# Sinkhorn-sorted attention and a gated MLP on one core: K of two batches mixed by 64x64 blocks in four tiles of the array, and a new order of the work

## The chip, the core and the metric

The kernel runs on one core of one Trainium2 chip. A core has a TensorE (PE, which multiplies; its weight loads are listed apart as PEld), a VectorE (DVE), a ScalarE (ACT), a GpSimd (POOL) and a SyncE (SP), which run side by side and wait for each other by semaphores. PE writes into PSUM, eight banks of 128 partitions x 512 floats; DVE and ACT read it. DMA queues move data between memory and the core's SBUF; loads here are issued by POOL, which casts float32 to bfloat16 on the way, and the others by SP and ACT. The metric is the device time of one execution, in microseconds (us), the median of several runs.

## What is computed

Four batches, 8 heads, 768 positions, 64 columns a head. `sort_net` gives an 8x8 matrix P per batch and head, which five Sinkhorn rounds normalise. P mixes the 8 blocks of 96 positions of K and V; attention then stays inside a block; the result goes through a gated MLP whose gate mixes positions.

```python
k_sorted = np.einsum('bhij,bhjcd->bhicd', P, k_b)      # likewise v_sorted
scores = scale * np.matmul(q_b, k_sb.transpose(0, 1, 2, 4, 3))   # 96x96 per block
attn = softmax(scores);  x = attn @ v_sb                # heads side by side: 768 x 512
h = np.maximum(x @ w_in, 0.0);  u, v = h[..., :512], h[..., 512:]
v_s = np.einsum('ts,bsd->btd', w_spatial, layernorm(v)) + b_spatial[None, :, None]
out = (u * v_s) @ w_out
```

## The kernel before

The work is cut into small steps, and one string, `ORDER`, says in which order they are emitted: `KT:3:D:0:1` is step KT in PSUM tile 3, its copy by DVE (A would be ACT), batch 0, head pair 1. Each engine and each queue does its part of the steps strictly in that order; nothing is rescheduled. PSUM tiles 0 to 3 are two banks each, and 10 to 17 are single banks (bank n - 10), so that 14 is the first bank of tile 2.

The steps that the change and the prediction speak of, with their lines:

- `L` (line 171) issues a load on POOL's queue. q, k and v of a batch are 128 partitions x 8 heads x 6 positions x 64 columns: partition p holds positions 6p to 6p + 5.
- `QC` (363) casts the first half of the first batch's q, which SP loads as float32. `QT` (330) turns q of a head pair by PE; for batches 2 and 3 `QP` (369) packs q and `QX` (380) turns it by DMA.
- `SK` (240) is a Sinkhorn round on DVE and ACT. `PR` (263) spreads P over partitions by PE, `P0` (278) on DVE and `PD` (290) on POOL multiply it with a mask into pd: for every head a 128x128 matrix that mixes the 8 blocks, since 128 partitions hold 8 blocks of 16.
- `KT` (402) mixes and turns K of a head pair: 12 matmuls (line 395) of 128 rows x 64 columns of weights (K) and 128 moving columns (pd). Two of them run at once, in the left and the right half of the array. `VT` (405) and `VB` (408) do that with V of batch 0, and turn it back into vb, position by partition.
- `VM` (418) mixes V of the other batches into vm, and `VC` (432) issues SP's DMAs that lay vm out as vb, one for each of the 8 blocks. There are two vb tiles, one for even batches and one for odd.
- `SC` (446) has the scores of a head pair and four blocks: 8 matmuls (454) of 64 rows, and ACT's exponential (459). `AT` (491) multiplies with vb (8 matmuls, 500) and DVE normalises (507, 508). `AT:1:1:0:0` is PSUM tile 1, batch 1, head pair 0, blocks 0 to 3; a last 1 means blocks 4 to 7.
- `XT`, `XD` turn x; `WT`, `WW` turn w_spatial; `VP`, `VH` (559) make the v half of the MLP, `ST`, `LN`, `LA` (581 to 599) its normalisation on DVE and ACT, `UP` (605) the u half, `SP` and `SH` (620, 676) the mixing of positions (PE, then DVE adds the bias), `GT`, `GH` the gate on DVE or POOL, `OP`, `OH` the last product, `OE`, `OI`, `OS`, `OJ` its way out. `CK`, `CF`, `LF` check that a short form of Sinkhorn and softmax was safe; a second path is there if not.

A KT is these lines of `mixed`:

```python
nc.tensor.matmul(
    t[hh * 64:hh * 64 + 64, g * 128:(g + 1) * 128],
    lhsT=st[x, b][:, 2 * hp + hh, g * D:(g + 1) * D], rhs=pd(b)[:, 2 * hp + hh, :],
    start=True, stop=True)
```

Of the kernel before, what the change touches and what calls it, by code (L numbers as in the profile page):

```python
# [30 lines left out]
AT:3:1:3:0 QP:A:2:2 AT:2:1:0:1 QP:A:2:1 SP:0:0:0 AT:1:1:1:1 SP:3:0:2 VM:2:A:2:2 XD:1:0 VM:0:A:2:1 GT:D:0:0 SP:1:0:1
VM:3:D:2:0 GT:P:0:1 VM:2:A:2:3 VH:10:A:1:0 ST:1:0 KT:1:A:2:0 KT:2:D:2:1 KT:3:A:2:3 QX:2:0:4 KT:0:D:2:2 XD:1:1
UP:1:A:1:1:0 VH:16:D:1:1 SC:2:2:2:0 SC:0:2:0:0 VC:2:0:4:0:4 ST:1:1 GT:P:0:2 SC:1:2:3:0 VH:17:D:1:3 L:wo UP:2:A:1:1:1
AT:0:2:2:0 VH:16:A:1:4 AT:1:2:0:0 GT:P:0:3 VH:17:D:1:5 SC:2:2:1:0 L:q:3:0:8 SC:0:2:0:1 SC:1:2:1:1 VH:16:A:1:2 ST:1:3
UP:2:A:1:0:0 ST:1:5 AT:0:2:3:0 ST:1:4 ST:1:2 UP:1:A:1:0:1 LN:1:0:6 OP:3:0:2:2 LA:1:5 LA:1:1 SC:2:2:3:1 L:v:3:0:8
SC:0:2:2:1 PD:3:4:8 LA:1:0 OP:1:0:4:2 PD:3:0:4 LA:1:3 LA:1:2 OE:A:0:2 LA:1:4 L:k:3:0:8 QP:D:3:0 VC:2:4:8:0:4 OE:A:0:4
AT:2:2:3:1 SP:0:1:3 QP:A:3:3 AT:3:2:1:0 AT:1:2:2:1 QP:A:3:1 SP:2:1:1 AT:0:2:1:1 QP:A:3:2 VM:3:A:3:1 OP:1:0:0:2
OE:D:0:0 OS:0:0:0:1:A OS:0:0:1:2:A VM:2:A:3:3 AT:3:2:0:1 SP:0:1:2 VM:1:A:3:0 GT:P:1:1 XD:2:0 VM:3:D:3:2 SP:2:1:0
VH:16:D:2:2 QX:3:0:4 KT:0:A:3:0 KT:1:D:3:2 KT:2:D:3:3 KT:3:A:3:1 XD:2:1 VH:10:D:2:0 SC:1:3:0:1 ST:2:2 SC:3:3:0:0
SC:2:3:3:1 VC:3:4:8:0:4 OS:0:4:0:1 OS:0:4:1:2 VH:11:D:2:4 VH:10:A:2:5 AT:1:3:0:1 GT:P:1:3 VH:16:D:2:3 ST:2:3 ST:2:5  # L40
GT:P:1:2 SC:2:3:1:1 SC:0:3:2:1 SC:1:3:1:0 VH:17:A:2:1 GT:D:1:0 UP:2:A:2:1:0 AT:0:3:2:1 UP:1:A:2:1:1 ST:2:1 AT:3:3:1:1
ST:2:4 AT:2:3:3:1 UP:0:A:2:0:1 ST:2:0 UP:1:A:2:0:0 VC:3:0:4:0:4 AT:3:3:0:0 LN:2:0:6 LA:2:2 OP:0:1:0:2 OE:A:1:0 LA:2:4
# [26 lines left out]
def kernel(  # L69
# [217 lines left out]
    def u_PC(eng):  # L287
        copy(eng, prep_sb, st["pr"])
# [560 lines left out]
```

## Time and profile before

| what | us |
|---|---|
| median of 3 runs | 150.17 |
| lowest and highest | 149.5, 150.21 |
| span of the profiled execution, first to last instruction | 147.7 |
| median less span | 2.5 |

The profiled execution's own time is given by its span; what lies around it is seen only against the timed runs, as the last row does. In the profile a row of the chain or of a timeline begins with the start in us from the span's start and the duration in us; then come the engine, the line and the operation. A line can be a helper's: L122 is every copy by ACT and L124 every copy by DVE. The duration of one matmul in a timeline includes its way through the array, so the pace of a stream of matmuls is read from the chain, whose pieces end where the next begins.

### The profile page before, as it was taken

The page shows a single profiled execution, that of the slowest core. Times are in us where ns is not written, and L with a number is a line of the kernel's source. Part 1 is how long each engine was busy: PE and PEld are TensorE (multiplying, and loading weights), DVE is VectorE, ACT ScalarE, POOL GpSimd, SP SyncE. Part 2 cuts the span into 40 slices and gives each one's busy share as a digit, 9 for nine tenths or more (in the row PEclk, how much of TensorE's full clock was granted, in tenths as well). Part 3 has the DMA queues.
Part 4 walks back from the last instruction along what each step waited for, and adds up shares of the span by engine and source line. Part 5 has one row for each costly group of instructions (what it writes and reads, how often), then busy time and mean ns, then how long its engine had stood idle before and what let it go on. Part 6 is the DMA issues. An engine that isn't in the chain of part 4 may idle for free.

```text
span 147.7 us, 4114 instructions
## 1 busy us (share of the span) xinstructions
PE 141.4 (96%) x1691; PEld 101.0 (68%) x1691; DVE 115.1 (78%) x263; ACT 85.2 (58%) x125; POOL 39.1 (26%) x44
## 2 busy tenths in 40 slices
PE   6997999999999999999999999999999999999991
PEld 2466777857776667776877678768866876854760
DVE  3878899979987978867869879899558989846741
ACT  5357998988789447658793328756640046160040
POOL 6701994410000006991002640000002100004630
PEclk9999999999999999999999999999999999999999
DMA  2999999999999999899999999503602507007856
GB/s 60 278 204 205 204 207 201 208 225 243 227 233 231 204 200 269 131 177 211 206 202 175 213 239 278 132 0 83 28 0 60 190 2 284 0 2 266 307 210 228
DMA packets 37013, 25.93 MB, mean 176 GB/s; under 512 B 16704, under 2 KB 34112, under 8 KB 36992
## 3 DMA queue, kind: packets, MB, share of 16 engines
q0 software_dynamic: 14432, 12.19, 51.9%
q1 hardware_dynamic: 21552, 11.88, 33.8%
q10 hardware_dynamic: 1008, 1.57, 2.8%
q8 instruction: 14, 0.23, 0.6%
q14 instruction: 7, 0.06, 0.1%
HBM read 24.78 MB, written 6.29 MB: 210 GB/s over the span
## 4 chain that ended last, share of the span: by engine, by line
PE 82%; DMA 8%; DVE 5%; POOL 2%; issue 1%; ACT 1%; POOLq 0%; DVEq 0%
PE ps L625 16%; PE ps L567 15%; PE ps L613 14%; PE ps L651 11%; DMA k_in<-in_k_dram 8%; PE ps L681 5%; PE ps L500 4%; PE ps L395 4%; PE ps L701 4%; PE ps L454 4%; PE ps L422 3%; DVE x_sb L508 2%; PE ps L326 1%; PE ps L536 1%; PE ps L530 1%; DVE vb L124 1%
## 5 line engine op out<-in xcount | busy, mean ns | idle before, releaser
L642 POOL TENSOR_TENSOR gt<-z,u_sb 128x768 bf16<-128x768 f32 x7 | 11.4, 1642 | 68.0 <-DVE z L631 54.7
L459 ACT ACTIVATE ex_all<-ps 96x768 bf16<-96x768 f32 x32 | 23.7, 805 | 5.0 <-PE ps L454 4.1
L625 PE MATMUL ps<-wspT,v_sb 128*128 128x384 bf16 x144 | 25.0, 326 | 0.0
L567 PE MATMUL ps<-w_in_sb,xT 128*128 128x256 bf16 (+1 forms) x176 | 23.8, 283 | 0.0
L613 PE MATMUL ps<-xT,w_in_sb 128*128 128x384 bf16 x128 | 23.0, 326 | 0.0
L128 ACT ACTIVATE u_sb<-ps 128x768 bf16<-128x768 f32 x16 | 13.0, 811 | 17.3 <-PE ps L613 17.2
L508 DVE TENSOR_TENSOR x_sb<-ps,rec_all 96x512 bf16<-96x512 f32 x32 | 22.0, 687 | 1.1
L625 PEld LDWEIGHTS <-v_sb 128*128 128x128 bf16 x144 | 13.5, 98 | 8.4
L567 PEld LDWEIGHTS <-xT 128*128 128x128 bf16 x176 | 16.2, 98 | 4.0
L651 PE MATMUL ps<-w_out_sb,gt 128*128 128x256 bf16 x144 | 16.9, 273 | 0.0
L613 PEld LDWEIGHTS <-w_in_sb 128*128 128x128 bf16 x128 | 12.0, 98 | 7.0
L587 DVE BATCH_NORM_STATS2 stats<-v_sb 128x6 f32<-128x512 bf16 x24 | 16.2, 675 | 0.6 <-ACT v_sb L128 0.5
L122 ACT COPY o_sb<-ps 128x1024 f32<-128x1024 f32 (+2 forms) x11 | 8.9, 830 | 12.6 <-PE ps L701 9.3
L631 DVE TENSOR_TENSOR z<-ps,b_bc 128x768 f32<-128x768 f32 x12 | 11.5, 954 | 5.9 <-PE ps L625 5.1
L651 PEld LDWEIGHTS <-gt 128*128 128x128 bf16 x144 | 13.8, 98 | 2.0
L500 PEld LDWEIGHTS <-ex_all 96*128 96x128 bf16 x256 | 11.1, 97 | 2.6
L500 PE MATMUL ps<-vb,ex_all 96*128 96x65 bf16 x256 | 12.4, 193 | 0.1
L122 ACT CAST vm<-ps 128x768 bf16<-128x768 f32 x9 | 6.8, 807 | 9.7 <-PE ps L422 6.6
L694 POOL TENSOR_TENSOR gt<-z,u_sb 128x512 bf16<-128x512 f32 (+1 forms) x5 | 5.2, 1046 | 21.5 <-DVE z L687 21.5
L507 DVE RECIPROCAL rec_all<-ps 96x8 f32<-96x8 f32 x32 | 6.3, 196 | 5.5 <-PE ps L500 5.3
L130 DVE TENSOR_SCALAR v_sb<-ps 128x512 bf16<-128x512 f32 (+1 forms) x12 | 8.7, 727 | 1.7 <-PE ps L567 1.5
L236 PE MATMUL ps<-warm 128*128 128x512 bf16 (+3 forms) x38 | 8.5, 386 | 1.3 <-DVE warm L210 1.3
(100 smaller groups left out, 199.9 us busy)
## 6 DMA issues: line engine op xcount, KB each, us to landing
v_in<-in_v_dram POOLq DMA_DIRECT2D x4, 768.0 KB, 16.0
k_in<-in_k_dram POOLq DMA_DIRECT2D x4, 768.0 KB, 14.9
vb<-vm SPq DMA_DIRECT2D x24, 99.0 KB, 4.8
q_in<-in_q_dram POOLq DMA_DIRECT2D x3, 768.0 KB, 11.6
out_dram<-o_sb SPq DMA_DIRECT2D x9, 256.0 KB, 2.3
out_dram<-o_sb SPq DMA_DIRECT2D x4, 512.0 KB, 5.9
out_dram<-o_sb ACTq DMA_DIRECT2D x5, 256.0 KB, 2.3
ws_in<-in_moe_w_spatial_dram POOLq DMA_DIRECT2D x2, 576.0 KB, 18.9
```

The costliest lines, as they stand in the source:

```text
L122: nc.scalar.copy(out=out, in_=in_)
L128: nc.scalar.activation(out=out, in_=in_, func=AF.Relu)
L459: nc.scalar.activation(out=e_tile(b, hp, ih).rearrange("p h (x g) -> p h x g", g=G), in_=t[0:BLK, :, 0:HW].rearrange("p h (g x) -> p h x g ...
L500: nc.tensor.matmul(t[:, hh, ii * VW:ii * VW + D + 1], lhsT=e[:, c:c + 128], rhs=vb[b % 2][:, ih * NI + ii, 2 * hp + hh, 0:D + 1], start=Tr ...
L508: nc.vector.tensor_mul(out=x_sb[:, hp].rearrange("p i (h d) -> p h i d", h=2), in0=tv[:, :, :, 0:D], in1=_raw_ap(rec, 0, [rec.ap[0], [NI, ...
L567: nc.tensor.matmul(t[:, x, c:c + DH // parts], lhsT=st["xT", b][:, n // 3, kc, (n % 3) * 128:(n % 3 + 1) * 128], rhs=w_in_sb[:, kc, DH + c ...
L587: nc.vector.bn_stats(out=stats, in_=st["v_sb", b, n])
L613: nc.tensor.matmul(t[:, x, 0:HW], lhsT=w_in_sb[:, kc, mc * 128:(mc + 1) * 128], rhs=st["xT", b][:, ih, kc, :], start=(kc == 0), stop=(kc = ...
L625: nc.tensor.matmul(t[:, x, 0:HW], lhsT=st["v_sb", b, n][:, mc * 128:(mc + 1) * 128], rhs=wspT[:, 3 * x:3 * x + 3, n, :], start=(n == 0), s ...
L631: nc.vector.tensor_add(out=z.rearrange("p (x c) -> p x c", x=2), in0=t[:, :, 0:HW], in1=b_bc.rearrange("p (x c) -> p x c", x=2),)
L642: eng.tensor_mul(out=gt, in0=st["z", b, mc], in1=u)
L651: nc.tensor.matmul(t[:, x, c:c + w], lhsT=st["gt", b, mc][:, (n0 + x) * 128:(n0 + x + 1) * 128], rhs=w_out_sb[:, mc, c:c + w], start=(mc = ...
```

## The change

Four things are changed.

1. K of batches 2 and 3 is loaded in another layout: a tile of 128 partitions holds two heads, 64 partitions each, with 12 positions per partition. A head is then mixed by a 64x64 matrix (`pn`, made by POOL in step `PN` from a smaller spread of P, steps `M8`, `PS`, `PY`), and step `KP` does two head pairs at once: 48 matmuls of 64 rows, 64 columns of weights and 64 moving columns, in the four quarters of the array. Four successive matmuls write four different PSUM banks. One KP takes the place of two KT. For odd head pairs the two heads stand in swapped halves, in q too, so their QP is two copies.
2. K of batch 0 is loaded ahead of V, with KT and the first scores ahead of VT.
3. `SH` can write its 512 columns in two parts.
4. `ORDER` is another throughout. Of its table two pieces:

```diff
-S0 TB CO LH:S:0 L:q:0:4:8 SK:0 ... BH ID IV:0 L:v:0:0:8 MC MA SK:1 DM:10:4:256 SK:2
-QC:A:0 SK:3 SK:4 QC:A:1 QT:10:A:0:2 IV:2 QT:11:A:0:3 ...
+S0 TB CO LH:S:0 SK:0 L:q:0:4:8 ... BH L:k:0:0:8 ID IV:0 MC MA M8 SK:1 DM:10:4:256
+SK:2 QC:D:0 SK:3 SK:4 IV:2 QT:11:A:0:0 QC:A:1 ...
```

The core of the rest:

```diff
+        if what == "k" and int(a[0]) >= KB:
+            b, lo, hi = (int(x) for x in a)
...
+            nc.gpsimd.dma_start(
+                out=st["k", b][:, lo:hi],
+                in_=_raw_ap(k, (b * H + 2 * lo) * S * D, [[GR * D, 128], [2 * S * D, hi - lo], [1, GR * D]]),
+            )
...
+    def u_PN(b, lo, hi):
...
+        nc.gpsimd.tensor_mul(
+            out=pn(b)[:, lo:hi].rearrange("p h (i t) -> p h i t", t=TR),
+            in0=_raw_ap(mask8, 0, [mask8.ap[0], [0, n], [0, NB], [1, TR]]),
+            in1=_raw_ap(prep8, (b - KB) * HP + lo, [prep8.ap[0], [1, n], [(B - KB) * HP, NB], [0, TR]]),
+        )
+
+    def half(b, hp, hh):
+        lo = 64 * (hh ^ (hp & 1) if b >= KB else hh)
+        return slice(lo, lo + 64)
...
+    def u_KP(ps0, ps1, eng, b, m):
+        b, m = int(b), int(m)
+        ts = [ps_tile(ps0), ps_tile(ps1)]
+        for n in range(GR):
+            for row in range(2):
+                g = (n + G * row) % GR
+                for o in range(2):
+                    rows = slice(64 * row, 64 * row + 64)
+                    nc.tensor.matmul(
+                        ts[o][half(b, o, row), g // G, (g % G) * 64:(g % G) * 64 + 64],
+                        lhsT=st["k", b][rows, 2 * m + o, g * D:(g + 1) * D], rhs=pn(b)[rows, 2 * m + o, :],
+                        start=True, stop=True,
+                    )
+        for o in range(2):
+            to = turned("kT", b, 2 * m + o)[:, 0:S].rearrange("p (x b g) -> p b x g", b=2, g=G)
+            copy(eng[o], to, ts[o][:, :, 0:HW].rearrange("p b (g x) -> p b x g", g=G))
```

Three places show what the new order moves. The first is ACT's queue in batch 0, from the last turns of q to the first copies of vm (`kt_all` is mixed K, `ex_all` the exponential of the scores, `vt_all` mixed V). Before:

```order
L122 COPY qT<-ps 128x768 x3
L122 CAST vt_all<-ps 128x768
L122 CAST prep_sb<-ps 128x256
L122 COPY vb_97<-ps 96x8x2x64
L122 CAST vt_all<-ps 128x768
L122 CAST kt_all<-ps 128x768 x2
L459 ACTIVATE ex_all<-ps 96x768 x7
```

And in the changed kernel (its line numbers are other ones):

```order
L125 COPY qT<-ps 128x768 x3
L125 CAST kt_all<-ps 128x768 x2
L529 ACTIVATE ex_all<-ps 96x768
L125 CAST vt_all<-ps 128x768
L529 ACTIVATE ex_all<-ps 96x768 x2
L125 CAST vt_all<-ps 128x768
L529 ACTIVATE ex_all<-ps 96x768 x3
L125 CAST vt_all<-ps 128x768
L529 ACTIVATE ex_all<-ps 96x768 x2
L125 CAST vm<-ps 128x2x6x64 x4
```

Mixed K comes first and V between the exponentials; before, V stood ahead of all of them.

The second place is PE's queue where vb of batch 1 is first read; the semaphores DMAHW2 to DMAHW7, then DMAHW0 and DMAHW1, are SP's eight VC in the order of issue. Before, behind a step VH, it is AT:1:1:0:0:

```order
L567 LDWEIGHTS xT
L567 MATMUL ps<-w_in_sb,xT 128x256
L500 LDWEIGHTS ex_all
L500 MATMUL ps<-vb_98,ex_all 128x65 [waits DMAHW2_49]
L500 LDWEIGHTS ex_all
L500 MATMUL ps<-vb_98,ex_all 128x65 [waits DMAHW3_49]
```

In the changed kernel this same step stands behind a VP and waits for the last four:

```order
L637 LDWEIGHTS xT
L637 MATMUL ps<-w_in_sb,xT 128x512
L570 LDWEIGHTS ex_all [waits DMAHW6_49]
L570 MATMUL ps<-vb_101,ex_all 128x65 [waits DVE_49]
L570 LDWEIGHTS ex_all
L570 MATMUL ps<-vb_101,ex_all 128x65 [waits DMAHW7_49]
L570 LDWEIGHTS ex_all
L570 MATMUL ps<-vb_101,ex_all 128x65 [waits DMAHW0_49]
```

The first four are waited for by AT:2:1:0:1; between the two stand another AT, a VH, a WW and a VP. VC has changed its order to blocks 4 to 7 and then 0 to 3.

The third place is DVE's queue ahead of SH in batch 3 (`BN_STATS` is ST, `TENSOR_SCALAR v_sb<-v_sb` is LA, `TENSOR_SCALAR u_sb<-ps` the relu of UP, `z` the bias of SH). Before, its end is:

```order
L587 BN_STATS stats<-v_sb 128x6 [waits Activation_49]
L588 BN_AGGR mv<-stats 128x2 [waits DVE_49]
L599 TENSOR_SCALAR v_sb<-v_sb,mv,rstd 128x512 [waits Activation_49]
L124 COPY o_sb<-ps 128x1024 [waits DMASW5_49,DMASW0_49,PE_49]
L599 TENSOR_SCALAR v_sb<-v_sb,mv,rstd 128x512
L599 TENSOR_SCALAR v_sb<-v_sb,mv,rstd 128x512 [waits DVE_49]
L599 TENSOR_SCALAR v_sb<-v_sb,mv,rstd 128x512 x3
L687 TENSOR_TENSOR z<-ps,b_bc 128x512 [waits PE_49,Pool_49]
```

In the changed kernel:

```order
L657 BN_STATS stats<-v_sb 128x6
L658 BN_AGGR mv<-stats 128x2 [waits DVE_49]
L133 TENSOR_SCALAR u_sb<-ps 128x2x384 [waits PE_49]
L824 TENSOR_LOAD flag [waits DVE_49]
L669 TENSOR_SCALAR v_sb<-v_sb,mv,rstd 128x512 [waits Activation_49]
L669 TENSOR_SCALAR v_sb<-v_sb,mv,rstd 128x512 [waits DVE_49]
L669 TENSOR_SCALAR v_sb<-v_sb,mv,rstd 128x512 x3
L127 COPY o_sb<-ps 128x1024 [waits DMASW0_49]
L133 TENSOR_SCALAR u_sb<-ps 128x2x384 [waits PE_49]
L669 TENSOR_SCALAR v_sb<-v_sb,mv,rstd 128x512
L759 TENSOR_TENSOR z<-ps,b_bc 128x512 [waits PE_49]
```

The relus of UP, which ACT did here, are now DVE's (four in all, two of them in these rows), and the last LA stands behind one of them.

More of the change, by code (lines that the diff above doesn't have):

```diff
@@ L285, in u_P0, with u_M8, u_PS, u_PY @@
         )
+    def u_M8():
+        nc.gpsimd.tensor_add(out=mask8, in0=m32[:, 0:TR], in1=m32[:, TR:TB])
+        nc.gpsimd.tensor_copy(out=spread8, in_=spread[:, :, 0:TR])
+    def u_PS(ps):
+        t = ps_tile(ps)[:, 0, 0:NB * (B - KB) * HP].rearrange("p (i y) -> p i y", i=NB)
+        parts = t.rearrange("p (k i) y -> p i k y", i=NI)
+        turned_p = p_t.rearrange("p (k y h) -> p h k y", k=2, h=2)
+        for i in range(NI):
+            for hh in range(2):
+                nc.tensor.matmul(
+                    parts[hh * 64:hh * 64 + 64, i], lhsT=spread8[:, i * NB:(i + 1) * NB].rearrange("p j t -> p (j t)"),
+                    rhs=turned_p[:, hh, :, KB * HP:], start=True, stop=True,
+                )
+        st["pr8"] = t
+    def u_PY(eng):
+        copy(eng, prep8, st["pr8"])
+    def pn(b):
+        if ("pn", b) not in st:
+            st["pn", b] = att.tile([128, HP, 64], BF16, name="pn", tag="pn", bufs=2)
+        return st["pn", b]
+    def u_PN(b, lo, hi):
+        b, lo, hi = int(b), int(lo), int(hi)
+        n = hi - lo
+        nc.gpsimd.tensor_mul(
[6 more added lines that the diff above has]
+        return slice(lo, lo + 64)
     def u_PC(eng):
@@ L374, in u_QP @@
                 "p (k g h d) -> p k g h d", k=HP, g=G, h=2)
-        copy(
-            eng, st["qp", b][:, hp].rearrange("p g h d -> p h g d"),
-            st["q", b][:, 2 * hp:2 * hp + 2].rearrange("p h (g d) -> p h g d", g=G),
-        )
+        to, of = st["qp", b][:, hp], st["q", b][:, 2 * hp:2 * hp + 2].rearrange("p h (g d) -> p h g d", g=G)
+        if half(b, hp, 0).start == 0:
+            copy(eng, to.rearrange("p g h d -> p h g d"), of)
+        else:
+            for hh in range(2):
+                copy(eng, to[:, :, 1 - hh], of[:, hh])
     def u_QX(b, lo, hi):
@@ L452, in u_SC @@
             for hh in range(2):
-                rows = slice(hh * 64, hh * 64 + 64)
+                rows = half(b, hp, hh)
                 nc.tensor.matmul(
```

125 lines of the change are left out of this document (72 added, 53 removed).

## The prediction

> **What bounds the kernel now.** I read the profile's page first, then the chain that ended last, then the DMA issues, and last the timelines of the first 40 us and of the tail. The page:
>
> ```profile
> span 147.7 us, 4114 instructions
> PE 141.4 (96%) x1691; PEld 101.0 (68%) x1691; DVE 115.1 (78%) x263; ACT 85.2 (58%) x125; POOL 39.1 (26%) x44
> ...
> PEclk9999999999999999999999999999999999999999
> DMA  2999999999999999899999999503602507007856
> ```
>
> TensorE is busy for 96% of the span at a full granted clock. The DMA row is the second thing to see: the DMA engines are full in the first 25 of 40 slices (to about 92 us), so until then data comes when the queues deliver it. The chain (start, duration, what) says which of the two sets the time where:
>
> ```profile
> 3.90 11.51 DMA k_in<-in_k_dram
> ...
> 24.00 0.81 ACT ex_all L459
> ...
> 27.68 0.79 PE ps L395 x24
> ...
> 36.71 0.33 PE ps L536 x6
> ...
> 37.91 0.48 PE ps L500 x16
> ...
> 41.24 0.28 PE ps L454 x8
> ...
> 42.93 0.24 PE ps L500 x8
> ...
> 44.18 0.45 PE ps L454 x16
> ...
> 56.10 0.87 PE ps L567 x8
> 56.98 1.46 PE ps L395 x48
> ...
> 60.72 0.62 PE ps L454 x24
> ...
> 62.31 1.30 PE ps L613 x8
> ...
> 79.54 1.75 PE ps L651 x16
> ...
> 131.41 7.80 PE ps L681 x48
> 139.21 5.22 PE ps L701 x36
> ```
>
> Up to 24.8 us the chain runs through DMA, DVE and ACT; from there to 144.43 every piece is PE, and no wait stands between them. So an edit acts through the work in PE's queue, or through a wait that PE meets. The piece at 37.91 begins with AT:1:1:0:0, the first step that reads vb of the second batch. It stands in both orders, and I count from it.
>
> **PE's work from AT:1:1:0:0 to the end.** These rows also price a change of tile shape. Scores (L454) take 0.28, 0.45 and 0.62 for 8, 16 and 24 matmuls: 0.17 per step, and 0.11 once per piece. K mixing (L395) takes 0.79 for 24 and 1.46 for 48: 0.335 per step of 12, and again 0.12 once. L500, whose neighbours have its own shape, takes 0.24 and 0.48, nothing once. So PE pays 0.11 to go to another tile shape. Counted along PE's instructions, the change takes 8 KT (-2.68) and 2 AT (-0.47) out of what follows AT:1:1:0:0, adds 3 WT (+1.0) and 1 VH (+0.87) there, takes 1 WW (two WT, -0.67) away, adds 0.06 in SH, 4 KP, and 6 changes of shape (28 for 22, +0.65).
>
> A KP has 48 matmuls of 64 columns in four tiles at once, 12 rounds of four. No such round is in the trace. Its nearest row is L500: 65 columns in 30 ns with the weights loaded behind, so 12 x 0.03 = 0.36 for a KP, and less is excluded, as four tiles at once can't stream 64 columns faster than the whole array takes 65. From above, if weight loads don't hide behind so short a stream, a round lasts like one of KT (0.335 / 6 = 0.056), 0.67, which is what the two KTs cost that it replaces. I take 0.40, near L500's row: 1.6 for four. The sum is -2.68 - 0.47 + 1.0 + 0.87 - 0.67 + 0.06 + 0.65 + 1.6 = +0.4 (0.2 to 1.5): behind AT:1:1:0:0 the change takes nothing off PE, since changes of shape and moved steps use up what the packing saves. The Trainium skill (TensorE: Matmul & The Clock Gate, LDWEIGHTS) gives a weight load as its columns over 1.2, 53 ns for 64; by that estimate a KP is 0.64 and the sum 1.4. No row here shows a load by itself.
>
> **When AT:1:1:0:0 can start.** SP's queue copies vb from vm in eight DMAs:
>
> ```profile
> 25.38 2.21 ACT L122 CAST vm<-ps 128x768 bf16<-128x768 f32 x3
> ...
> 27.67 5.21 SPq L435 DMA_DIRECT2D vb<-vm  x8
> ```
>
> The DMA view at the fourth and at the eighth of these issues (the last figure is us from issue to landing):
>
> ```profile
> vb<-vm SPq DMA_DIRECT2D x1, 99.0 KB, 7.1
> ```
> ```profile
> vb<-vm SPq DMA_DIRECT2D x1, 99.0 KB, 8.8
> ```
>
> The issues stand 0.65 apart, so the fourth landed at 29.7 + 7.1 = 36.8 and the eighth at 32.3 + 8.8 = 41.1: 9.1 and 13.4 us after the first issue, among full DMA engines. Now that is in time: AT:1:1:0:0 needs the first four at 37.9, and the first step that reads the others is the piece at 42.93. The change issues blocks 4 to 7 first, puts two steps that read them (AT:2:1:0:1, AT:1:1:1:1) ahead of AT:1:1:0:0, and this one then needs the last four. By the prices above PE has 11.1 us of work from the last VM to AT:1:1:0:0, and vm's copy on ACT ends 1 us after that VM; the last four need 13.4 from there.
>
> So vm's end decides. The start, in ACT's, PE's and DVE's timelines:
>
> ```profile
> 9.63 0.82 ACT L122 CAST q_in<-q 128x768 bf16<-128x768 f32 x1
> 10.35 2.17 ACT L122 COPY qT<-ps 128x768 bf16<-128x768 bf16 x3
> ...
> 11.51 0.28 PE L267 MATMUL ps<-p_t,spread 32*128 32x64 bf16 x4 [0.52 <-DVE mask L224]
> ...
> 11.90 0.75 DVE L281 TENSOR_TENSOR pd<-mask,ps 128x256 bf16<-128x256 bf16 x2 [0.38 <-ACT qT L122]
> ...
> 12.37 0.86 PE L395 MATMUL ps<-pd,v_in 128*64 128x128 bf16 x24
> ...
> 17.74 5.04 ACT L459 ACTIVATE ex_all<-ps 96x768 bf16<-96x768 f32 x7
> ```
>
> And one group (the last figure ahead of the second bar is the mean in ns):
>
> ```profile
> L124 DVE CAST kt_all<-ps 128x768 bf16<-128x768 f32 x7 | 6.5, 947 | 0.5 <-PE ps L395 0.4
> ```
>
> A cast of q goes onto DVE between two Sinkhorn rounds. The nearest row is this cast from PSUM, 0.95 for as many columns; part of it lies where DVE would wait for ACT's exponential, so Sinkhorn ends 0 to 0.9 later, say 0.1. The other cast (0.82) now stands on ACT behind a qT copy (0.7), and the turn of q that PE does ahead of PR waits for it: 9.7 + 0.7 + 0.8 = 11.2, the turn, and PR at about 11.8 for 11.51. The first KT needs DVE's second P0, not its first (0.4): 13.0 for 12.37. From 13.6 on ACT has 2 kt, 8 exponentials, 3 vt and 4 vm to do up to vm's end, 17 at 0.73 (2.21 / 3): 12.4. To this come about 0.4 where V of the first batch lands (at K's old place, 3.90 + 11.51 = 15.4) and 0.8 where VMs share one PSUM tile: 27.2, for 25.38 + 2.21 = 27.6 now. The exponentials begin near 15.1 for 17.74, but the work put ahead of vm uses that up. Of the rest, M8 and PN lie on POOL (26% busy), PY (64 columns) and the halved QP on DVE and ACT between waits, PS's 8 short matmuls ahead of P0's end, and POOL issues K of the second batch behind PD at about 16, with two loads still queued ahead: at nothing, all.
>
> The eight land 12.5 to 13.4 after 27.3, at 39.8 to 40.7; I take 40.5, by the row of the same stretch, since the same loads share the engines. PE alone would come at 38.4. Its own gate is K of the second batch, now sixth in POOL's queue, where q stood (timeline, then the DMA view at this issue):
>
> ```profile
> 16.18 0.94 POOL L177 DMA_DIRECT2D q_in<-in_q_dram  x1
> ```
> ```profile
> q_in<-in_q_dram POOLq DMA_DIRECT2D x1, 768.0 KB, 11.6
> ```
>
> That is 27.8, then 10.3 of work to AT:1:1:0:0, and 0.3 for a copy that VP waits for. Behind the waiting AT stand all later steps of PE. Late next is q of the third batch, now behind wu and v on POOL, near 50, but then wanted no earlier.
>
> **The tail.** DVE's load ahead of SH:
>
> ```profile
> 114.50 0.41 DVE L733 TENSOR_REDUCE ends<-rec_all 96x1 f32<-96x256 f32 x1
> ...
> 116.26 0.96 DVE L631 TENSOR_TENSOR z<-ps,b_bc 128x768 f32<-128x768 f32 x1
> ...
> 118.45 0.95 DVE L642 TENSOR_TENSOR gt<-z,u_sb 128x768 bf16<-128x768 f32 x1
> 119.31 0.68 DVE L130 TENSOR_SCALAR v_sb<-ps 128x512 bf16<-128x512 f32 x1
> ...
> 122.06 0.69 DVE L587 BATCH_NORM_STATS2 stats<-v_sb 128x6 f32<-128x512 bf16 x1 [0.20 <-ACT v_sb L128]
> ...
> 122.89 0.66 DVE L587 BATCH_NORM_STATS2 stats<-v_sb 128x6 f32<-128x512 bf16 x1
> ...
> 127.88 1.22 DVE L124 COPY o_sb<-ps 128x1024 f32<-128x1024 f32 x1
> 129.02 1.70 DVE L599 TENSOR_SCALAR v_sb<-v_sb,mv,rstd 128x512 bf16<-128x512 bf16 x5
> ```
>
> Now LA ends at 130.7 and SH starts at 131.41. In the new order DVE has from the z of SP:1:2:1 on: that z (0.9), the check (114.50 to 116.26, 1.76), two gates (0.86 each, 118.45 to 119.31), the flag (0.3), six ST (0.8), four relus of UP (0.86, a cast's 0.947 less the overlap), one of VH (0.6), six LA (0.33) and the copy (1.15): 16.7. PE has from the end of SP:1:2:1 to SH 6 tiles of VH (0.87), 4 UP (1.30), 3 OP (1.75) and 0.25: 15.9, and 0.33 more until SH's fourth matmul wants v_sb from LA:3:3, DVE's last. So SH waits 0.5 (0 to 1.2).
>
> **The sum.** (40.5 - 37.9) + 0.4 + 0.5 = +3.5 on the span of 147.7: 151.2. What lies around it is taken from the median, 150.17 - 147.7 = 2.5: 153.7. The wait errs towards less, if at all, so I forecast 153.4.
>
> **The rivals.** (a) vb is in time, if all eight land in 11 us and not in 13.4: then AT:1:1:0:0 starts at 38.4, and it is 0.5 + 0.4 + 0.5: 151.5, at the low ends 150.3. Against it: the full DMA row. (b) PE issues packed matmuls one by one at a pace of its own. The shortest here is that of scores, 0.17 for 8, 21 ns each; at that pace a KP lasts 48 x 0.021 = 1.0 and 4 x 0.6 comes on top of the forecast: 155.8. Against it: scores stream 96 columns in pairs, and half of L500's 30 ns x 96 / 65 is 22 by itself. The Trainium skill (TensorE: Matmul & The Clock Gate, Wait — 56ns, not 53.3ns?) has matmul starts never below about 25 ns; by it a KP would be 1.2. The 21 ns are already below that. (c) Faster: ACT paces the first stage, and its exponentials start 2.6 earlier; if the three loads behind 15.4 also run at 3.7 each, and not at (27.8 - 15.4) / 3 = 4.1, K of the second batch lands at 26.5, PE comes at 36.8, and vb, from vm's end at 26, is there by then. That is -1.1 + 0.2 with DVE's tail covered: 149.3. It decides where AT:1:1:0:0 starts ahead of 37. For it: DVE and ACT carry the chain until 24.8; against it: q took until 27.8 in this place.
>
> **How the numbers follow.** Chances: forecast 0.58, (a) 0.21, (b) 0.07, (c) 0.14. A measurement can tell about 0.5%, 0.75 us. Faster is (c), 0.14; the same is the low end of (a), 0.08; slower the rest, 0.78. The range leaves out (b) and most of (c): from (a)'s low end, 150.3, to vb at 40.7 (+0.2) with a KP of 0.55 (+0.6) and a tail of 1.2 (+0.7), 155.2.
>
> **What would show it.** Right: PE waits for DMA vb at L570 between 35 and 41 us, AT:1:1:0:0 starts after 39, and a KP takes 0.35 to 0.5. Wrong: no wait on vb, vm's end ahead of 26, or KPs of a microsecond. A first SH piece longer than 1.3 us shows the tail.

## The result and the profile after

The changed kernel takes 158.06 us (median of 4 runs, 157.38 to 158.74), the kernel before 150.15: a ratio of 1.055 with a 95% interval of 1.050 to 1.059. The sign was forecast, the size was not: 7.9 us and not 3.2, outside the range. Medians here and in the table of the experiments are of each kernel's fast runs, the profiled one among them, so one run each of `after_all_three` and `after_covered`, more than 1.5% above the fastest, is not in them; the ratios go by the runs beside the profiled one. The profiled execution has a span of 156.2 for 147.7. The page of the changed kernel:

```profile
span 156.2 us, 4384 instructions
...
PE 144.0 (92%) x1817; PEld 103.1 (66%) x1819; DVE 117.9 (76%) x272; ACT 82.0 (53%) x121; POOL 41.1 (26%) x48
...
PEclk9999999999999999999999999999999999999999
DMA  3999999999999959999991998813154120149356
...
PE 66%; DVE 15%; DMA 10%; SPq 3%; issue 2%; ACT 2%; DVEq 0%
```

TensorE's share fell from 96% to 92%. The chain that ended last was PE alone from 24.8 to 144.4 us before; now it leaves PE again behind 27 us. The chain (start, duration, what):

```profile
27.12 0.81 ACT vm L125
...
28.01 0.72 SPq L505
...
28.77 1.40 SPq L505
...
33.46 8.34 DMA vb<-vm
...
41.84 0.31 PE ps L570 x5
...
60.64 0.51 PE ps L466 x48
...
67.31 6.73 DMA vb<-vm
...
74.09 0.31 PE ps L570 x5
...
138.69 0.33 DVE v_sb L669
...
139.06 6.41 PE ps L753 x57
...
146.27 0.42 DVE z L759
...
146.73 0.81 PE ps L753 x6
147.55 5.22 PE ps L773 x36
```

Behind the first stage it leaves PE at three places: for vb of batch 1 (8.34 us from the last of SP's issues to its landing), for vb of batch 2 (6.73), and in the tail for DVE, once for the normalised v_sb and once for a bias addition, z. (As in the diff, batches count from 0 here: 0 to 3. The recorded expectations below count them from 1.) PE's own timeline shows what stood still (in brackets the idle time ahead of the row and what ended it):

```profile
35.62 0.29 PE L570 MATMUL ps<-vb,ex_all 96*128 96x65 bf16 x2
37.53 0.19 PE L570 MATMUL ps<-vb,ex_all 96*128 96x65 bf16 x1 [1.62 <-DMA vb<-vm]
38.30 0.55 PE L570 MATMUL ps<-vb,ex_all 96*128 96x65 bf16 x13 [0.58 <-DMA vb<-vm]
...
41.84 0.31 PE L570 MATMUL ps<-vb,ex_all 96*128 96x65 bf16 x5 [0.48 <-DMA vb<-vm]
...
71.06 0.31 PE L570 MATMUL ps<-vb,ex_all 96*128 96x65 bf16 x5 [1.03 <-DMA vb<-vm]
...
74.09 0.31 PE L570 MATMUL ps<-vb,ex_all 96*128 96x65 bf16 x5 [0.61 <-DMA vb<-vm]
```

A matmul's duration includes its way through the array, so I count the loss between starts, less 0.03 us for each matmul's own pace: the AT of batch 1 lost 3.2 us there (1.78, 0.74 and 0.65) and those of batch 2 2.5 (1.19, 0.48 and 0.78). Some expectations below have 3.4 and 2.7 for them, with the matmuls' own pace in it. Points that both chains have:

| PE starts | before | after | later by |
|---|---|---|---|
| AT:1:1:0:0, its last part after | 37.91 | 41.84 | 3.9 |
| K mixing of batch 2 | 56.98 | 60.64 | 3.7 |
| the last product, OH | 139.21 | 147.55 | 8.3 |

From the first row to the last the new order takes 4.4 us more: 2.5 for vb of batch 2, 1.2 in the tail (0.4 at v_sb, 0.8 at z), and 0.8 that is left for work, changes of tile shape and smaller waits.

### The profile page after: what moved, and what is told of

Its sections match the earlier page's. It is cut to its first block, busy times and chain, and to the rows that moved or that the text cites. A ratio compares the mean times of both kernels' runs of the same rounds, so it can differ in the third digit from the quotient of the medians.

```text
span 156.2 us, 4384 instructions
## 1 busy us (share of the span) xinstructions
PE 144.0 (92%) x1817; PEld 103.1 (66%) x1819; DVE 117.9 (76%) x272; ACT 82.0 (53%) x121; POOL 41.1 (26%) x48
## 4 chain that ended last, share of the span: by engine, by line
PE 66%; DVE 15%; DMA 10%; SPq 3%; issue 2%; ACT 2%; DVEq 0%
PE ps L695 15%; DMA vb<-vm 10%; PE ps L683 8%; PE ps L637 7%; PE ps L721 7%; PE ps L250 6%; PE ps L753 5%; PE ps L570 4%; SPq L505 3%; PE ps L773 3%; PE ps L524 3%; DVE stats L657 2%; DVE u_sb L133 2%; PE ps L492 2%; PE ps L483 1%
## 5 line engine op out<-in xcount | busy, mean ns | idle before, releaser
L712 POOL TENSOR_TENSOR gt<-z,u_sb 128x768 bf16<-128x768 f32 x8 | 13.0, 1640 | 70.4 <-DVE rec_all L577 38.3
L529 ACT ACTIVATE ex_all<-ps 96x768 bf16<-96x768 f32 x32 | 24.3, 805 | 3.6 <-PE ps L524 3.6
L570 PE MATMUL ps<-vb,ex_all 96*128 96x65 bf16 x256 | 13.2, 193 | 4.7 <-DMA vb<-vm 4.6
L570 PEld LDWEIGHTS <-ex_all 96*128 96x128 bf16 x256 | 11.4, 97 | 8.2 <-issue 5.6
L131 ACT ACTIVATE v_sb<-ps 128x512 bf16<-128x512 f32 (+1 forms) x14 | 8.8, 629 | 12.6 <-PE ps L637 12.3
L131 ACT ACTIVATE u_sb<-ps 128x768 bf16<-128x768 f32 x11 | 8.9, 812 | 7.0 <-PE ps L683 7.0
L125 ACT CAST vm<-ps 128x768 bf16<-128x768 f32 x10 | 7.7, 802 | 7.9 <-PE ps L492 7.8
L250 PE MATMUL ps<-warm 128*128 128x512 bf16 (+3 forms) x38 | 9.5, 415 | 1.3 <-DVE warm L224 1.3
L125 ACT CAST kt_all<-ps 128x768 bf16<-128x768 f32 x10 | 7.8, 809 | 5.3 <-PE ps L466 5.1
```

The lines of the kernel that those rows point to most:

```text
L125: nc.scalar.copy(out=out, in_=in_)
L131: nc.scalar.activation(out=out, in_=in_, func=AF.Relu)
L250: nc.tensor.matmul(t[:, 0, 0:int(w)], lhsT=warm[:, 0:128], rhs=warm[:, 0:int(w)], start=True, stop=True)
L529: nc.scalar.activation(out=e_tile(b, hp, ih).rearrange("p h (x g) -> p h x g", g=G), in_=t[0:BLK, :, 0:HW].rearrange("p h (g x) -> p h x g ...
L570: nc.tensor.matmul(t[:, hh, ii * VW:ii * VW + D + 1], lhsT=e[:, c:c + 128], rhs=vb[b % 2][:, ih * NI + ii, 2 * hp + hh, 0:D + 1], start=Tr ...
L712: eng.tensor_mul(out=gt, in0=st["z", b, mc], in1=u)
```

## The experiments

Eighteen kernels ran: my first theory, that each of these waits is a loss that an edit at its place gives back, failed again and again. Medians, with the ratio to the kernel before (149.8 to 150.3 beside them) and its interval:

| kernel | us | ratio |
|---|---|---|
| before_packed | 164.33 | 1.099 (1.095 to 1.103) |
| after_unpacked | 157.61 | 1.052 (1.045 to 1.059) |
| after_late_at | 160.14 | 1.068 (1.059 to 1.077) |
| after_relu_act | 158.32 | 1.060 (1.053 to 1.068) |
| after_loads_moved | 161.77 | 1.080 (1.075 to 1.084) |
| after_at_spread | 157.20 | 1.050 (1.048 to 1.052) |
| after_all_three | 158.88 | 1.067 (1.060 to 1.074) |
| before_packed_wo | 166.41 | 1.114 (1.107 to 1.120) |
| after_wu_first | 158.33 | 1.053 (1.045 to 1.060) |
| after_loads_last | 158.81 | 1.057 (1.048 to 1.067) |
| after_covered | 160.02 | 1.063 (1.052 to 1.073) |
| after_covered_unpacked | 158.74 | 1.057 (1.049 to 1.065) |
| after_loads_last_v | 157.54 | 1.051 (1.047 to 1.056) |
| after_covered2 | 157.37 | 1.051 (1.048 to 1.055) |
| after_covered2_unpacked | 156.76 | 1.046 (1.044 to 1.048) |
| before_packed2 | 152.96 | 1.021 (1.018 to 1.024) |
| after_old_vb | 154.85 | 1.035 (1.032 to 1.037) |
| after_old_vb_unpacked | 154.55 | 1.033 (1.031 to 1.035) |

None comes near the kernel before.

### Order or packing?

`after_unpacked` keeps the new order and mixes K by KT throughout:

```diff
-KP:3:1:AD:2:1 VH:11:A:1:0 KP:3:2:AA:2:0
+KT:3:A:2:2 KT:1:D:2:3 VH:11:A:1:0 KT:2:A:2:1 KT:3:A:2:0
...
-KP:2:3:AD:3:1
+KT:2:A:3:2 KT:3:D:3:3
...
-KP:3:0:AD:3:0
+KT:3:A:3:0 KT:0:D:3:1
```

> The changed kernel with KT in the place of KP and without PS, PY, PN and M8: the new order alone. If the new order makes the loss, it stays slow: 158.0 to 159.2, the packed form having saved 0 to 1.2 of TensorE. If the packing makes it, the time falls to 152 or less.

157.61: without any KP the loss is still there, so it comes with the new order (and with changes 2 and 3, which this kernel keeps). `before_packed` does the opposite, the old order with KP:

```diff
-KT:1:A:2:0 KT:2:D:2:1 KT:3:A:2:3 QX:2:0:4 KT:0:D:2:2
+KP:1:2:AD:2:0 QX:2:0:4 KP:0:3:DA:2:1
...
-KT:0:A:3:0 KT:1:D:3:2 KT:2:D:3:3 KT:3:A:3:1
+KP:0:3:AA:3:0 KP:1:2:DD:3:1
```

> The kernel before with the packed mixing alone: its own order, K of batches 3 and 4 by KP in the place of the eight KT, with the small products and masks that KP needs. If the packing itself is cheap (8 KT x 0.335 us = 2.68 out, 4 KP x 0.51 us with their change of shape = 2.04 in, some 0.4 for PS), the time is 149.9, between 149.2 and 150.6, the same as before. If the packing is what made the changed kernel slow (its changes of shape, its extra q copies, its work on VectorE and GpSimd), it is 152 to 156.

164.33, 14.6 us over a kernel that does the same but for KP. I had expected no change. Its trace names a transfer, not TensorE. PE's timeline, then the clock in two stretches (the column of 1.00 and 0.57 is the granted clock), then PE's first row behind the branch to the last part:

```profile
66.88 0.19 PE L570 MATMUL ps<-vb,ex_all 96*128 96x65 bf16 x1 [2.88 <-DMA vb<-vm]
68.58 0.31 PE L570 MATMUL ps<-vb,ex_all 96*128 96x65 bf16 x5 [1.51 <-DMA vb<-vm]
```
```profile
66.00:69.00 3.00, 0.61 (x9) 0.48 (x9) 0.00 (x0) 0.00 (x0) 1.75 (x3) 1.00 1.14 209
69.00:73.00 4.00, 4.00 (x48) 2.99 (x45) 2.59 (x6) 0.91 (x2) 0.00 (x0) 0.57 1.28 221
```
```profile
151.33 7.03 PE L773 MATMUL ps<-w_out_sb,gt 128*128 128x512 bf16 x36 [3.53 <-issue]
```

Three mishaps: 4.4 us of waiting for vb of batch 2, a clock of about half for 3.4 us right behind it, and 3.5 us of idle PE at its branch to the last part, which lasted 5.1 us with a fetch of 16 KB of code inside, and a granted clock of 0.50 once more behind that. Why vb came late is in the issues. Before:

```profile
57.59 5.70 SPq L435 DMA_DIRECT2D vb<-vm  x8
```
```profile
59.79 0.82 POOL L194 DMA_DIRECT2D w_out_sb<-in_moe_w_out_dram  x1
```

In `before_packed` the eight issues begin at 58.18 and are spread over 7.13 us, and POOL's load of w_out stands at 60.02. The DMA views at the second and at the third of these issues (59.5 and 60.17; the last figure is us from issue to landing):

```profile
vb<-vm SPq DMA_DIRECT2D x1, 99.0 KB, 3.1
```
```profile
vb<-vm SPq DMA_DIRECT2D x1, 99.0 KB, 6.7
```

A piece issued ahead of the load lands in 3.1, one issued behind it in 6.7. Before, four pieces were ahead of w_out, the fourth (59.74) by 0.05 us; here two are, and the third is issued 0.15 us behind the start of w_out's issue. The other profiles of this case tell the same of vb of batch 2: a piece takes 2.7 to 4.4 us ahead of POOL's next load, in all twenty, and 6.6 to 8.8 behind that load's issue, in the fourteen that have such pieces; those issued while the load's own issue lasts (0.8 us) lie between, 3.0 to 7.6, up to 4.2 where it had begun less than 0.1 us before. It is also the second loss of the changed kernel: there QX holds SP's queue until 61.4 and one piece is ahead.

```profile
57.85 3.54 SPq L435 DMA_TRANSPOSE qT<-qp  x1
61.50 6.39 SPq L505 DMA_DIRECT2D vb<-vm  x8
```
```profile
62.15 0.81 POOL L208 DMA_DIRECT2D w_out_sb<-in_moe_w_out_dram  x1
```

Its first piece landed in 3.2 us, the second, issued 0.04 us behind the start of w_out's issue, in 4.2, the third in 6.6. The Trainium skill (DMA: Bandwidth & Descriptors, Queues, rings and completion order) says that the write that counts a transfer as done lands only after every earlier write of the same DMA engine, whatever queue it came from. The order of the landings agrees with that, but the rule alone is not the delay, for the data of the pieces are late too. Between 65.6 and 67.1 us, with the third piece issued and not landed, no packet of SP's queue (q1) begins; in 66 to 67 us all packets that begin are POOL's (q0):

```profile
DMA packets 169, 0.17 MB, mean 173 GB/s; under 512 B 0, under 2 KB 169, under 8 KB 169
...
q0 software_dynamic: 169, 0.17, 121.3%
```

The third piece's data move from 67.1 to 68.7, and it has landed at 69.5. What holds the packets back no run here shows.

### One wait at a time

`after_late_at` puts three AT of batch 1 behind other work, `after_relu_act` gives DVE's four relus of the tail back to ACT:

```diff
-SC:0:1:2:0 AT:2:1:0:1 AT:1:1:1:1 ... VP:15:A:0:1 AT:1:1:0:0 WT:14:D:3 ... VH:11:D:0:2
+SC:0:1:2:0 ... VP:15:A:0:1 WT:14:D:3 ... VH:11:D:0:2 AT:2:1:0:1 AT:1:1:1:1 AT:1:1:0:0
```
```diff
-UP:1:D:3:0:1 ... UP:0:D:3:1:1 ... UP:0:D:3:0:0 ... UP:0:D:3:1:0
+UP:1:A:3:0:1 ... UP:0:A:3:1:1 ... UP:0:A:3:0:0 ... UP:0:A:3:1:0
```

> The changed kernel with the first three AT of batch 2 behind VP:15, WT:14, WT:17 and VH:11, so that TensorE has some 5 us of other work while the eight vb transfers land. If the wait for vb of batch 2 is real loss, 2.6 to 3.5 us go: 154.5 to 155.5. If the transfers are hidden anyway, or the same time comes back as a later wait for vb of batch 3, it stays at 157 to 158.

> The changed kernel with the four UP relus of batch 4 on ScalarE again. If VectorE's queue holds the first SH of the tail, 1.0 to 1.5 us go: 156.5 to 157.0. If ScalarE then takes the place (its OE copies and exps behind the relus), or something else holds the tail, it stays within 0.4 of 158.0.

160.14 and 158.32: neither gains. In the first, vb is there, but the AT now stand close together, and two of them share PSUM tile 1:

```profile
42.78 0.40 PE L570 MATMUL ps<-vb,ex_all 96*128 96x65 bf16 x8 [2.04 <-DVE x_sb L578]
44.19 1.15 PE L524 MATMUL ps<-qT,kt_all 64*128 64x96 bf16 x24 [1.01 <-DVE x_sb L578]
```

The wait for a transfer has become one of 3 us for DVE to empty a bank. In the second, SH no longer waits for v_sb, but it still waits 0.7 for z, because the last SH uses bank 13 again while DVE has a gate (1.36 us) to do first: the relus weren't all of the tail.

### The loads

`after_loads_moved` lets w_out load 30 us earlier, behind k of batch 2, and puts one more gate on POOL ahead of batch 3's loads; `before_packed_wo` does the first with `before_packed`. `after_at_spread` gives the AT of batch 1 other work between them; `after_all_three` is both and the relus on ACT.

```diff
-L:k:2:0:4 ... GT:D:0:2 ... GT:P:0:1 ... SC:1:2:3:0 L:wo
+L:k:2:0:4 L:wo ... GT:P:0:1 GT:P:0:2 ... SC:1:2:3:0
```
```diff
-VP:15:A:0:1 AT:1:1:0:0 WT:14:D:3 L:wu WT:17:A:0 VH:11:D:0:2 SC:1:1:2:1 ...
+VP:15:A:0:1 WT:14:D:3 L:wu VH:11:D:0:2 AT:2:1:0:1 AT:1:1:1:1 WT:10:A:0 SC:3:1:2:1 ... WT:11:A:2 AT:2:1:0:0 SC:1:1:3:1 ...
```

> The changed kernel with the load of w_out put behind k of batch 3 (it then fills the stretch from 54 us in which no load runs) and one product gt moved from VectorE to GpSimd ahead of q, k and v of batch 4. Theory one: vb of batch 3 comes late because its pieces are issued behind a load of 1.5 MB. Then the first four pieces land by 67, the two waits of 1.2 us at 70 and 73 us go, and the time is 155.0 to 156.2. Rival: the pieces are late because QX holds SyncE's queue until 61.4, whatever the loads do; then the waits stay and the time is 157.2 to 158.5.

> The changed kernel with the first AT of batch 2 behind VP:15, WT:14 and VH:11 and with other work (WT, SC) between them on other banks, so that none waits for VectorE to empty a bank. Theory one: the wait for vb of batch 2 is loss that other work can cover: 2.5 to 3.5 us go, 154.6 to 155.6. Rival: what is saved here only comes back as a longer wait for vb of batch 3, whose landing is set by the loads: 157 to 158.5.

> The changed kernel with both of these and the four UP relus of batch 4 on ScalarE. Theory one: all waits but the packing's changes of shape and the fetch of TensorE's code in the tail go, 151.0 to 153.0. Rival: the loss lies in the order as such (more changes of shape, VectorE's queue), and the time stays above 154.5.

> The kernel before with the packing, and the load of w_out behind k of batch 3. The run before it, with w_out where it stood, waited 4.7 us for vb of batch 3, since two of its eight pieces were issued ahead of that load where four were in the kernel before, and 2 us more at half clock right behind it; 3.5 us of it were TensorE's branch in the tail and 1.7 half clock behind that. Theory one: the first two go and the branch stays, 157.0 to 158.5 (or 152 if the branch goes too). Rival: the pieces come late for the time that the packing takes on SyncE or VectorE, and the time stays at 163 to 165.

(The profile gives w_out as 512 KB in SBUF; the size in the first expectation was wrong.) Only `after_at_spread` came out lower, by 0.9 of the 3 expected, and its interval overlaps the changed kernel's: it now waits at several places for 0.2 to 0.4 us each, for ACT and DVE, and the AT of batch 2 still wait for vb. `after_all_three` was forecast at 151 to 153; PE still waits 2.1 us for vb of batch 2 there. In `after_loads_moved` five pieces went ahead of the next load, of q, and the sixth 0.1 us behind the start of its issue; the six landed by 69.7, but PE wanted all eight, and the last two were behind it:

```profile
74.97 0.19 PE L570 MATMUL ps<-vb,ex_all 96*128 96x65 bf16 x1 [1.78 <-DMA vb<-vm]
76.26 0.31 PE L570 MATMUL ps<-vb,ex_all 96*128 96x65 bf16 x5 [1.10 <-DMA vb<-vm]
```

The sixth took 3.0 from issue to landing, the seventh 7.6. So what landed late was again what was issued behind a load, and the rival (QX) fell, while the forecast of the time failed. With w_out early a second thing came: the DMA that turns x (XD) then runs beside the load, 9.4 us from issue to landing in `after_all_three` for 4.7 in the changed kernel, and 7.2 in `before_packed_wo`, where PE waited 1.2 us for it. That kernel, forecast at 157 to 158.5, also kept its other two waits: with q's load at 62.15, two pieces of vb were ahead of it and PE waited 3.4 us, and the branch took 5.1 again. The stretch without loads near 54 us was not free.

`after_loads_last` keeps w_out where it was and puts POOL's own work (two gates, PD, PN) ahead of all four loads, so that they are issued from 67.1 on; `after_loads_last_v` also loads v of batch 3 ahead of k.

```diff
-GT:D:0:0 VH:10:A:1:5 GT:D:0:2 ... GT:P:0:1 ST:1:3 ... PD:3:4:8 SC:1:2:3:0 L:wo
+VH:10:A:1:5 ... GT:P:0:1 GT:P:0:0 GT:P:0:2 ST:1:3 ... PD:3:0:4 PD:3:4:8 PN:3:0:4 SC:1:2:3:0 L:wo
```
```diff
-L:k:3:0:4 LA:1:0 ... L:v:3:0:8 QP:D:3:1
+L:v:3:0:8 LA:1:0 ... L:k:3:0:4 QP:D:3:1
```

> The changed kernel with GpSimd's work put in another order: two gt products from VectorE, PD and PN of batch 4 stand ahead of the loads of w_out and of q, k, v of batch 4, so that these are issued from about 67 us, behind all eight pieces of vb of batch 3. Theory: a piece issued ahead of a load lands some 3 us after its issue, one issued behind it some 7 us; all eight land by 70.5, the two waits of 1.2 us at 70 to 74 us go, and the time is 155.2 to 156.4. Rival: the later loads are waited for in their turn (w_out by the first OP, v of batch 4 by VM), and the time is 157.5 to 160.

> As after_loads_last, with V of batch 4 loaded ahead of its K. There all vb of batch 3 came in time, and the wait moved to V of batch 4 (landed 87.5, wanted at 84 by VM). With V one load of 4 us sooner it lands near 83.5 and that wait of 2 us goes: 156.0 to 157.2. Rival: the wait moves on again, to K of batch 4 or to the output's transfers: 158 or more.

All eight pieces are in by 69.6, the last 2.8 after its issue, and no AT of batch 2 waits. But the four loads need some 20 us one behind the other, and v of batch 3, the last, is wanted first:

```profile
87.68 0.81 PE L491 MATMUL ps<-v_in,pd 128*128 128x384 bf16 x4 [1.77 <-DMA v_in<-in_v_dram]
```

158.81: the rival. With v ahead of k that wait went and 157.54 came, 0.5 less than the changed kernel, which is inside the intervals; w_out is now waited for (0.7), and of the waits for vb of batch 1 two are still there (0.31 and 1.35), with a clock of 0.50 behind them.

### The cover of the first wait

In the kernel before, w_u landed at 37.94 and four UP of 1.3 us stood among the AT of batch 1; vb's last piece was no earlier there (41.1). In the new order w_u lands at 42.3. `after_wu_first` loads it first and takes two UP ahead; `after_covered` adds the edit of `after_loads_last`; `after_covered2` also uses other banks there and loads v ahead of k.

```diff
-AT:2:1:0:1 AT:1:1:1:1 L:wsb ... L:wsa WW:0:A:4 VP:15:A:0:1 AT:1:1:0:0 WT:14:D:3 L:wu ...
+L:wu ... L:wsb VP:15:A:0:1 UP:1:A:0:0:1 L:wsa AT:2:1:0:1 WW:0:A:4 AT:1:1:1:1 UP:3:A:0:0:0 SC:1:1:2:1 ... AT:2:1:0:0 ...
```

> The changed kernel with w_u loaded ahead of both parts of w_spatial, so that it lands near 35 and not at 42.3 us, and two UP of batch 1 between the AT that wait for vb of batch 2. Theory: the kernel before hid the same late vb (its last piece landed at 41.1) behind UP work, which the new order took away by loading w_u last; given back, the waits of 3.4 us at 35 to 42 us go, and 2 to 3 us of it reach the end: 155.0 to 156.2. Rival: SyncE's queue and the loads set the pace anyway, and what is gained is waited for again in batch 3: 157 to 158.5.

> Both together: 152.5 to 154.0 if the two waits are separate losses and nothing else becomes late, which leaves the tail (1.2 us with the fetch of TensorE's code in it), the packing and the changes of shape. Above 155.5 the loss is not these waits.

> The same with KT in the place of KP, without PS, PY, PN and M8. With TensorE's waits gone the packing shows what it is worth: 4 x (2 x 0.335 - 0.51) = 0.64 us less the 12 small products of PS, so this should be 0.2 to 0.8 slower than the packed form. If it is faster, the packing costs in another place (the two q copies, GpSimd's and VectorE's work for it).

> As after_covered, with V of batch 4 ahead of K and with the WT, SC and AT of batch 2 on other banks, since there three WT in one bank and two AT in one waited 2.8 us for ScalarE and VectorE. Theory: with vb, loads and banks out of the way the new order reaches 152.5 to 154.5. Rival: above 157, the loss is of another kind.

> The same with KT for KP: 0.2 to 0.8 slower than after_covered2 if the packing saves TensorE what its rows say; the same or faster if its copies, masks and changes of shape cost what it saves.

158.33, 160.02, 158.74, 157.37 and 156.76. The vb wait of batch 1 went below 1 us, as meant, and the next ones came at once: in `after_wu_first` WT for ACT (0.44 and 0.99) and AT for DVE (1.02); in `after_covered` v of batch 3 again (2.00, and a half clock behind it); in `after_covered2` this:

```profile
51.10 0.48 PE L490 MATMUL ps<-v_in,pd 128*128 128x384 bf16 x2 [1.35 <-DVE x_sb L576]
```

Between 28 and 50 us of the kernel before PE is busy all the time, DVE 86%, ACT 85%, and the DMA engines are full. That leaves little room there, and in each of these runs the edit of one queue's order was met by a wait for another.

### The packing by itself

`before_packed2` has KP in the old order with an UP between the first two, on other banks, w_out behind one more gate, and 24 more narrow warm-up products, which move PE's branch in its code:

```diff
-KP:1:2:AD:2:0 QX:2:0:4 KP:0:3:DA:2:1 XD:1:1 UP:1:A:1:1:0
+KP:1:2:AD:2:1 QX:2:0:4 UP:3:A:1:1:0 KP:0:1:DA:2:0 XD:1:1
...
-VH:17:D:1:3 L:wo ... GT:P:0:3
+VH:17:D:1:3 ... GT:P:0:3 L:wo
...
-DM:13:10:192
+DM:13:34:48
```

> The kernel before with the packing, now with an UP between the two KP of batch 3, banks 2 and 3 exchanged behind them, the KP of batch 4 in the order in which their banks come free, the load of w_out behind one more product on GpSimd so that four pieces of vb are issued ahead of it again, and 24 more narrow warm-up products, which move TensorE's branch in its code. If the packing itself is cheap: 149.3 to 150.8. If it costs by itself, 152 or more; the branch alone, if it still waits for its code, adds 3.5 to 5.

152.96: 11.4 us less than `before_packed` by placing alone, with neither the vb wait of batch 2 nor the branch's, and still 3.2 more than the kernel before. What stands still in its trace: 0.7 for xT, 0.8 for vm's copy on ACT, 0.35 for a bank, 0.9 for vb of batch 3. Its QX starts at 53.27 for 51.80 before, but not for ACT's packing of q, which ends at 50.81, though each half of an odd head pair takes 0.51 to 0.52 there and the whole took 0.83. QX stands behind the first turn of x, which begins 0.8 later (50.92 for 50.08) and holds SP's queue 2.23 us for 1.61.

`after_old_vb` leaves every instruction where it is; only the data of two batches' AT is other data, so that no transfer is waited for:

```diff
-rhs=vb[b % 2][...]
+rhs=vb[(b - 1 if b in (1, 2) else b) % 2][...]
```

> The changed kernel, whose AT of batches 2 and 3 read the other vb tile, that of the batch before, so that none of them waits for the eight transfers, which still run (the output of these two batches is made from the wrong V). If the vb waits are the loss, 3.4 us at 35 to 42 us and 2.7 us at 70 to 74 us go: 151.5 to 153.0. If other waits stand right behind them (banks, ScalarE, loads), less goes: 154 to 156. If they are hidden by something else on the path, 157 to 158.

> The same without the packing. If the packing saves TensorE what its rows say (0.64 us less 0.3 to 0.5 for PS), 0.1 to 0.4 slower than the packed form; by the two pairs measured so far (0.45 and 0.6 faster without it), 0.4 to 0.7 faster.

154.85 and 154.55. PE's busy time in 28 to 50 us, in the changed kernel and with the old vb (us, then PE's busy time):

```profile
28.00:50.00 22.00, 19.04 (x313) 13.89 (x311) 16.65 (x38) 16.24 (x24) 3.94 (x5) 1.00 1.22 228
```
```profile
28.00:50.00 22.00, 21.32 (x335) 15.30 (x336) 18.57 (x43) 17.94 (x26) 3.94 (x5) 1.00 1.22 228
```

So the vb waits carry 3.2 us of the 7.9, not the 5.6 that they show: when they go, the loads behind them are as late as before (v of batch 3 lands at 83.1, in the changed kernel at 83.4) and are met sooner.

```profile
83.16 0.81 PE L492 MATMUL ps<-v_in,pd 128*128 128x384 bf16 x4 [0.95 <-DMA v_in<-in_v_dram]
```

This run also shows that vb of batch 2 isn't late because the stage ahead of it is. Nothing waits for vb of batch 1 here, and still w_out's load comes behind the first piece (timeline, then the DMA view at the third issue):

```profile
59.57 6.62 SPq L505 DMA_DIRECT2D vb<-vm  x8
```
```profile
59.95 0.80 POOL L208 DMA_DIRECT2D w_out_sb<-in_moe_w_out_dram  x1
```
```profile
vb<-vm SPq DMA_DIRECT2D x1, 99.0 KB, 8.5
```

And the packing: four pairs, alike but for it, are 158.06 and 157.61, 160.02 and 158.74, 157.37 and 156.76, 154.85 and 154.55. The packed kernel is the slower one each time, by 0.3 to 1.3 us. Within a pair the intervals overlap or nearly touch, so what is sure is only that it gains nothing.

## Why the prediction was wrong

**When AT:1:1:0:0 can start: the mechanism held, the term was too small.** PE waits for vb at L570 between 35 and 41 us, as said. vm's end was forecast for 27.2 and came at 27.93 (27.12 + 0.81); the second of SP's issues took 1.40 and not 0.65; the last piece landed 8.3 after its issue, near the 8.8 used. 41.84, not 40.5: 3.9 and not 2.6.

**The step that failed: "Late next is q of the third batch, ... but then wanted no earlier."** It looked for what comes late behind the first wait and found only q. The wait for vb of the third batch (batch 2 here), 2.5 us, has no term in the sum at all, and among the things put "at nothing, all" is "the halved QP on DVE and ACT between waits". SP's queue wasn't followed into this stage. Before, ACT has packed q by 49.8, QX stands between the two turns of x, and four pieces of vb go out ahead of w_out:

```profile
51.80 4.27 SPq L382 DMA_TRANSPOSE qT<-qp  x1
```

In the new order QX stands behind both turns, and its last copy of q, now DVE's, ends at 57.69; so QX holds SP's queue from 57.85 to 61.39, although vm's last copy has ended at 60.29. The first piece goes out 3.9 us later than before (61.50 for 57.59), but w_out only 2.4 later (62.15 for 59.79). So three pieces of the first four are no longer ahead of it, and the third and the fourth take 6.6 and 7.5 us for 3.0 and 3.2 before. The margin, 59.74 against 59.79, stood in the trace before. That the stage began late isn't the reason: in `after_old_vb`, without the first wait, the first piece is still 2.0 later than before and w_out only 0.2. The wait goes when the loads are put behind (`after_loads_last`); whether SP's side of the crossing or POOL's is the cause, no run splits.

**PE's work behind it: right.** +0.4 (0.2 to 1.5) was forecast, 0.8 is left for it and for small waits. A KP takes 0.51 in the chain with its change of shape, forecast 0.40 and 0.11. Rival (b) falls: 0.51 / 48 is 11 ns for one matmul with its weights, so four quarters do work at once. Both rules of the Trainium skill weighed there (TensorE: Matmul & The Clock Gate, LDWEIGHTS and Wait — 56ns, not 53.3ns?) would have made it longer, 0.64 by a weight load of 53 ns and 1.2 by starts of 25 ns; the measured 0.51 is below both, so neither holds as it stands for four quarters at once. That the packing saves nothing held too, by four pairs of runs. Which of its side costs uses up the rest (PS, the two q copies, changes of shape, a KP's wait for a bank, 0.35 in `before_packed2`) isn't settled.

**The tail: half of it.** SH waits 0.4 for LA:3:3, with 0.5 forecast; the other 0.8, bank 13 used again while DVE has a gate before the z that empties it, was not looked for. Moving the relus to ACT took the first away and gave nothing measurable, so it isn't shown that either of them is worth its length.

**The sum.** 3.9 + 2.5 + 1.2 + 0.8 is, unrounded, 8.3 of the 8.5 by which the span grew. What the prediction had (2.6 + 0.4 + 0.5 = 3.5) was 3.9 + 0.8 + 0.4 = 5.1 in fact; the 2.5 for vb of batch 2 and 0.8 at bank 13 were not thought of. But these are waits as they show, and the runs say that they don't add: without both vb waits 4.7 us of the loss remain. By the traces that is V of batch 3 (1.0), the tail (1.2), some 1.7 in small waits between 28 and 51 us (for DVE, for PSUM banks and, once, 0.4 for w_u), and work; no run took these away without putting others in their place, so this part is argued and not shown.

## What to carry to other kernels

When an edit makes one stage late, follow every queue into the next stage, with the loads of other queues that it then meets: here a transfer that took 3.2 us when it was issued 0.05 us ahead of a big load took 7.5 behind it. A wait's length in a profile isn't what its removal gives: here 5.6 us of waits were worth 3.2. Taking the wait away with other data and no move of any instruction is the test for it; where work was moved by hand, other waits came. And an order that was fitted to its load times is part of the kernel: a small saving on one engine was worth nothing here where one queue moved past a neighbour.

## What was not expected of the hardware

- An SBUF transfer of 99 KB (vb of batch 2) takes 2.7 to 4.4 us from issue to landing ahead of POOL's next load and 6.6 to 8.8 behind it, in the fourteen profiles that have both. With no load running (vb of batch 3) it takes 2.7 to 4.3, in all twenty.
- In eight of the twenty profiles the granted clock fell to 0.50 for 3.41 us (once 6.83) behind a wait of PE; half clock for 3.41 us costs up to 1.7 us. It came behind waits of 2.88 and 1.51 us (`before_packed`), but also of 0.31 and 1.35 (`after_loads_last_v`), and it didn't come behind 1.62, 0.58 and 0.48 in the changed kernel's profile. So the length of the wait alone doesn't tell; some timed runs of the changed kernel have a mean clock of 0.985 to 0.989. The Trainium skill (TensorE: Matmul & The Clock Gate, Part 1: The HAM clock gate) has half clock until a window of 3.4 us was busy, and the length agrees.
- PE's branch to the last part took 0.48 us in eighteen kernels and 5.1 in the two that have 3491 PE instructions (matmuls and weight loads) ahead of it in the trace (3283 to 3349 and 3537 to 3557 in the others), with the fetch of the next 16 KB of code inside. The Trainium skill (Advanced Engine Details and Errata, ISA Cache) gives lines of 16 KB for 256 instructions, which fits the size fetched; where in a line the branch must not stand wasn't tried.
